# A list schedule that knows TensorE's tiling: each change of mode is charged, the mode at hand is preferred, and the order is drawn up anew

## The chip, the core and the metric

The kernel runs on one core of a Trainium2 chip. The metric is the device time of one launch in microseconds, 538.26 us in the median of three runs before the change. TensorE (PE in the profile, PEld its weight load), VectorE (DVE), ScalarE (ACT), GpSimd (POOL) and SyncE (SP, which issues the transfers) run side by side, each through its own list of instructions in the order in which the program gives them, and wait for one another by semaphores.

## What is computed

Shapes are 4 batches, 8 heads, 768 tokens, head size 48; the model width is 384 and the hidden width 1536. Cut to what matters, the reference is

```python
f = 1.0 / (1.0 + np.exp(-f_logit))
for t in range(S):                                   # attention with a gated state of 48x48
    state = f[:, :, t, :, None] * state + np.einsum('bhd,bhe->bhde', k[:, :, t], v[:, :, t])
    y[:, :, t] = np.einsum('bhd,bhde->bhe', q[:, :, t], state)
x = y.transpose(0, 2, 1, 3).reshape(B, S, H * D)
gate = sigmoid(sum(conv_w[k] * xp[:, k:k + S, :] for k in range(5)))   # causal, 5 taps
x = (gate * (x @ w_val)) @ w_out
xn = (x - mean) / sqrt(var + 1e-6) * g_ln
out = x + relu(xn @ w_ch1) @ w_ch2
```

The weights come in as 64-bit floats and are turned into pairs of 32-bit parts on the chip.

## The kernel before

The work is cut into 24 tiles of 128 tokens for the attention and 12 groups of 256 tokens for the dense layers. Every dense product is split into a high and a low part and made of three matmuls (`mm3`), in the form F32R: val (`ps<-xh,wv`), x1 (`ps<-wo,gh`), c1 (`ps<-nh,w`, 128x256) and c2 (`ps<-w,hidden`, 128x384). Of a tile of the attention TensorE does four things, each one block of instructions that the planner moves as a whole:

- T: transposes against an identity, `ps<-ident,kt` (and, ahead of the dense layer, `ps<-ident,xn`), 128 rows by 128 columns;
- a: `ps<-mv,kt`, scores of a chunk of 64 tokens, 48 rows by 64 columns of the array;
- d: `ps<-st,kn`, what a chunk adds to the state, 64 rows by 48 columns;
- y: `ps<-mv,st`, the output, 112 or 128 rows by 48 columns.

a, d and y use a part of the array only, and set TensorE to another tiling than T and the dense matmuls do. By the planner's classes a and d are one mode (at most 64 rows), y is a second, everything else is mode 0. Around these blocks DVE makes gates and running products (`gs`, `ft`, `kt`, `mv`, in `prep`), ACT copies the transposed keys (`kn`) and the scores, POOL masks the scores (`mv<-mv`). After d the state goes on through DVE (`sn<-sd,ps`), POOL (`sd<-sn,fc`) and a copy (`st<-sd`), and y of the same tile needs that copy.

Nothing of the order is written out by hand. `Kernel.record` records some 2,900 units (a block each) twice, and `Plan.schedule` sets the order: `forward` is a list scheduler which at each step takes the unit that can start first, and among equals the one of lowest rank. Ranks come from a backward pass, and the table `MOVED` then shifts the ranks of runs of units: (first unit, how many, by how much). Costs come from `price`, `transfer` and `wait`. In the old model every block on TensorE that isn't F32R pays `SWITCH` (0.12) once, whatever ran before it, and the transposes pay it too. The same order of one list then holds for all engines, the transfers on SP among them; places in PSUM (8 banks) are handed out as the order goes.

A word on stages: up to its first c1 matmul TensorE does seven tiles of the attention and one group of val and x1 besides transposes (128 rows of its list); from there the list mixes c1 and c2 of a group with the attention, val and x1 of later groups. Up to tile 7 (`TURNED`) q, k and f are transposed on TensorE (`ps<-ident,raw_f` and so on), later on DVE.

Of the kernel before, what the change touches and what calls it, by code (L numbers as in the profile page):

```python
# [49 lines left out]
FRONT = (-5, -4, -4, -2, -2, -1)  # L50
BIAS = 0.3
COLD = 1.25
WARM = 1.03
SWITCH = 0.12
TURNED = 8
REBIAS = 2.0**-112
TINY = 2.0**-60
# [5 lines left out]
FLIGHT = 8  # L63

MOVED = (
# [8 lines left out]
)  # L74


# [31 lines left out]
class Unit:  # L108


    def __init__(self, engine):
        self.costs = dict.fromkeys(engine.split("|"), 0.0)
        self.engine = next(iter(self.costs))
        self.calls = []
        self.delay = self.margin = 0.0
        self.deps = set()
        self.opens = None
        self.uses = set()
        self.port = False

# [12 lines left out]
class Plan:  # L133
# [43 lines left out]
    def record(self, engine, method, args, kw):  # L177
# [25 lines left out]
        for x, writes in [(x, False) for x in ins] + ([(out, True)] if on_chip(out) else []):  # L203
            r = self.region(x)
            if isinstance(r.name, int) and r.name not in u.uses:
                if not self.users[r.name]:
                    u.opens = r.name
                else:
                    u.deps.add(self.users[r.name][0])
                u.uses.add(r.name)  # L210
                self.users[r.name].append(me)
            ws, rs = self.access.setdefault(r.name, ([], []))
            for at, box in ws + (rs if writes else []):
                if at != me and (r.meets(box) or self.collide(r, at, u)):
                    first.deps.add(at)
            if writes:
                ws[:] = [(a, b) for a, b in ws if not r.covers(b)]
                rs[:] = [(a, b) for a, b in rs if not r.covers(b)]
                ws.append((me, r.box))
            elif (me, r.box) not in rs[-4:]:  # L220
                rs.append((me, r.box))
        if engine == "sync":
            return
        n = 1
        for _, k in out.ap[1:]:
            n *= k
        if engine == "tensor" and not u.costs["tensor"] and ins[0].dtype != F32R:
            u.costs["tensor"] = SWITCH
        wide = [x for x in ins if x.space != PSUM and x.ap[-1][1] > 1]
        single = method in ("tensor_scalar", "tensor_copy", "copy", "shifted") and out.space != PSUM  # L230
        u.port = method != "memset" and (len(wide) > 1 or (bool(wide) and (single or "gpsimd" in u.costs)))
# [13 lines left out]
    def price(self, engine, method, out, ins, n, args, kw):  # L245
        if engine == "tensor":
            if method == "transpose":
                return 0.105 * self.slow
            if ins[0].dtype == F32R:
                return (0.436e-3 * n + 0.006) * self.slow  # L250
            return (0.056 if n > D else 0.043) * self.slow
# [35 lines left out]
    def transfer(self, issued, u, out, in_):  # L287

        n = size = mybir.dt.size(out.dtype)
        for _, k in out.ap:  # L290
            n *= k
        run = size * min(out.ap[-1][1], in_.ap[-1][1])
        local = out.space == in_.space
        issued.costs = {"sync": 0.63 if out.ap[0][1] == 64 or local else 0.47}
        issued.delay = 0.5
        issued.margin = 0.0 if local else MARGIN
        u.costs = {"wire": n / run * (11.0 + (0.0595 if run < 1024 else 0.053 if run < 2048 else 0.0705) * run) / 16e3}
        u.delay = 1.2
        u.deps.add(len(self.units) - 1)

# [37 lines left out]
    def forward(self, deps, users, rank):  # L338
# [11 lines left out]
        homes = {}  # L350
        held = [len(x) for x in self.users]
        ends = [0.0] * len(held)

        def start(i, e):
            u = units[i]
            t = max(free[e], ready[i])
            if u.port and e in port:
                t = max(t, port[other[e]])
            if u.opens is not None:
                first = sorted(banks.values())  # L360
                spare = 1 if e == "vector" else 0
                t = max(t, first[spare]) if len(first) > spare else NEVER
            if e == "sync":
                t = max(t, free["wire"] - BACKLOG)
# [17 lines left out]
        while len(order) < len(units):  # L382
            best = None
            for e in ENGINES:
                for i in waiting[e]:
                    t = (start(i, e), ready[i] if e == "wire" else rank[i])
                    if (best is None or t < best[0]) and fits(i, e):
                        best = (t, i, e)
            (t, _), i, e = best
# [4 lines left out]
                waiting[x].remove(i)  # L394
            u.engine = e
            order.append(i)
            end[i] = free[e] = t + u.costs[e]
            if e == "sync":
                sent.append(i + 1)
            if u.port and e in port:  # L400
                port[e] = end[i] + 0.05
            if u.opens is not None:
                homes[u.opens] = min(banks, key=banks.get)
                del banks[homes[u.opens]]
            for r in u.uses:
                held[r] -= 1
                ends[r] = max(ends[r], end[i] + 0.17)
# [823 lines left out]
```

## Time and profile before

| | |
|---|---|
| median of three runs | 538.26 us (537.22 to 538.60) |
| the profiled execution | 538.87 us, of which its instructions span 537.2 us |
| mean granted TensorE clock | 0.99 |
| busy share of the span | PE 93%, PEld 89%, DVE 69%, ACT 50%, POOL 32% |
| costliest group | c1 `ps<-nh,w_hi`, 432 matmuls, 123.5 us busy |

Read a matmul's cost from the distance between two starts, not from its own duration: matmuls overlap in the array, a c1 matmul is shown with 0.28 us and the next one starts 0.11 us later. A timeline row `x32` stands for 32 instructions in a row of one kind; for a, d and y they are the 16 products of a block, each of which runs as two instructions on the chip.

### The profile page before, as it was taken

What the parts mean: (1) busy time and instruction counts of PE and PEld (TensorE: products, weight loads), DVE (VectorE), ACT (ScalarE), POOL (GpSimd) and SP (SyncE); (2) the same over time, 40 slices, a digit from 0 to 9 for tenths busy, and PEclk for the clock granted to TensorE, in tenths of its full rate; (3) what the DMA queues carried; (4) which work ended last, traced back from release to release, by engine and by line L of the source; (5) the groups of instructions that cost most, each with busy time, mean ns of one, the idle gap of its engine ahead of it and who ended that gap; (6) DMA issues with size and microseconds to landing.
All of it is one profiled execution on the core that took longest, in us unless ns stands there. A gap on an engine that the chain in (4) does not pass through costs nothing.

```text
span 537.2 us, 13413 instructions
## 1 busy us (share of the span) xinstructions
PE 501.3 (93%) x5272; PEld 477.9 (89%) x5272; DVE 369.1 (69%) x737; ACT 270.6 (50%) x591; POOL 169.5 (32%) x312
## 2 busy tenths in 40 slices
PE   2987689999999999999999999999999999999994
PEld 1776579999999999999989999999989999999993
DVE  5898989999884975874889733985793542543411
ACT  2598879995472453453486222543552542512210
POOL 3365676245340422230277001231421431300000
PEclk9998989999999999999999999999999999999998
DMA  6985786973454234133143610162110100000001
GB/s 137 177 172 106 190 214 173 234 227 83 103 145 94 51 85 92 39 100 70 38 114 73 149 47 1 31 156 60 24 39 9 23 31 2 9 31 1 29 1 35
DMA packets 94560, 45.60 MB, mean 85 GB/s; under 512 B 56341, under 2 KB 94485, under 8 KB 94490
## 3 DMA queue, kind: packets, MB, share of 16 engines
q1 hardware_dynamic: 94490, 44.67, 34.8%
q8 instruction: 43, 0.70, 0.6%
q14 instruction: 27, 0.22, 0.2%
HBM read 38.75 MB, written 4.72 MB: 81 GB/s over the span
## 4 chain that ended last, share of the span: by engine, by line
PE 71%; DVE 12%; DMA 4%; POOL 4%; ACT 3%; issue 2%; SPq 2%; DVEq 0%; POOLq 0%; ACTq 0%
PE ps L466 71%; DVE ps L466 4%; SPq L466 2%; POOL rs L466 2%; DVE mv L466 2%; DMA raw_q<-in_q 1%; DVE wt L466 1%; DMA xt<-x 1%; DMA stage<-in_moe_w_ch 1%; DVE gs L466 1%; ACT xn L466 1%; DVE bns L466 1%; DMA raw_f<-in_f_logit 1%; DMA out_x<-x 1%; DVE nl L466 1%
## 5 line engine op out<-in xcount | busy, mean ns | idle before, releaser
L466 PE MATMUL ps<-nh,w_hi 128*128 128x256 f32 x432 | 123.5, 286 | 0.4 <-DVE nl L466 0.3
L466 PE MATMUL ps<-nl,w_hi 128*128 128x256 f32 x432 | 121.1, 280 | 0.4 <-DVE nl L466 0.3
L466 PE MATMUL ps<-nh,w_lo 128*128 128x256 f32 x432 | 120.9, 280 | 0.0
L466 PE MATMUL ps<-w_hi,hidden_hi 128*128 128x384 f32 x288 | 99.3, 345 | 0.0
L466 DVE SCALAR_TENSOR_TENSOR hidden_lo<-ps,hidden_hi 128x512 fp32r<-128x512 f32 x72 | 49.2, 684 | 70.3 <-ACT hidden_hi L466 70.2
L466 PE MATMUL ps<-w_hi,hidden_lo 128*128 128x384 f32 x288 | 96.9, 337 | 0.0
L466 PE MATMUL ps<-w_lo,hidden_hi 128*128 128x384 f32 x288 | 96.8, 336 | 0.0
L466 ACT ACTIVATE hidden_hi<-ps 128x512 fp32r<-128x512 f32 x72 | 42.9, 595 | 85.7 <-PE ps L466 84.4
L466 PEld LDWEIGHTS ps<-nh,w_hi 128*128 128x128 f32 x432 | 81.3, 188 | 1.8 <-DVE nl L466 0.5
L466 PEld LDWEIGHTS ps<-nh,w_lo 128*128 128x128 f32 x432 | 82.1, 190 | 0.0
L466 PEld LDWEIGHTS ps<-nl,w_hi 128*128 128x128 f32 x432 | 81.2, 188 | 0.9 <-DVE nl L466 0.9
L466 DVE SCALAR_TENSOR_TENSOR ps<-xt,convw,ps 128x256 f32<-128x256 f32 x144 | 65.7, 483 | 3.5 <-ACT ps L466 1.8
L466 POOL TENSOR_SCALAR_AFFINE_SELECT mv<-mv 64x512 f32<-64x512 f32 x48 | 32.2, 671 | 86.6 <-ACT mv L466 84.9
L466 PEld LDWEIGHTS ps<-w_hi,hidden_hi 128*128 128x128 f32 x288 | 54.1, 188 | 1.1
L466 PEld LDWEIGHTS ps<-w_lo,hidden_hi 128*128 128x128 f32 x288 | 54.2, 188 | 0.0
L466 PEld LDWEIGHTS ps<-w_hi,hidden_lo 128*128 128x128 f32 x288 | 54.1, 188 | 0.0
L466 POOL TENSOR_TENSOR sd<-sn,fc 112x192 f32<-112x192 f32 x43 | 22.7, 529 | 69.8 <-DVE sn L466 54.9
L466 ACT COPY kn<-ps 64x192 f32<-64x192 f32 x96 | 30.1, 313 | 14.1 <-PE ps L466 12.9
L466 DVE TENSOR_TENSOR_SCAN gs<-ps,ends 128x511 f32<-128x511 f32 x24 | 29.1, 1214 | 9.3 <-ACT ps L466 8.9
L466 DVE TENSOR_TENSOR mv<-ps,ft 64x512 f32<-64x512 f32 x48 | 33.0, 688 | 2.5 <-PE ps L466 1.0
L466 PE MATMUL ps<-xh,wv_hi 128*128 128x256 f32 x108 | 32.7, 302 | 0.9 <-DVE gt L466 0.9
L466 PE MATMUL ps<-xl,wv_hi 128*128 128x256 f32 x108 | 31.4, 291 | 0.0
(102 smaller groups left out, 993.8 us busy)
## 6 DMA issues: line engine op xcount, KB each, us to landing
stage<-in_moe_w_ch SPq DMA_DIRECT2D x24, 384.0 KB, 4.5
st<-in_v SPq DMA_DIRECT2D x96, 48.0 KB, 2.5
out_x<-x SPq DMA_DIRECT2D x24, 192.0 KB, 1.9
raw_f<-in_f_logit SPq DMA_DIRECT2D x32, 96.0 KB, 2.3
raw_k<-in_k SPq DMA_DIRECT2D x32, 96.0 KB, 2.3
raw_q<-in_q SPq DMA_DIRECT2D x32, 96.0 KB, 2.4
raw_f<-in_f_logit SPq DMA_DIRECT2D x32, 80.0 KB, 2.2
raw_k<-in_k SPq DMA_DIRECT2D x32, 80.0 KB, 2.4
```

The costliest lines, as they stand in the source:

```text
L466: getattr(getattr(self.nc, engine), method)(*args, **kw)
```

## The change

The planner now carries the mode at hand through the forward pass. A block of a or d has mode 1, of y mode 2, all else 0, and a block whose mode differs from that of the block before it on TensorE pays 0.117 (into mode 0) or 0.092. Besides, the rank by which TensorE's blocks are compared gets `STAY` (3.0) added where the block would change the mode. `WARM`, the factor on all TensorE prices after the prologue, goes from 1.03 to 1.01, a transpose from 0.105 to 0.102; a transfer's price is divided by 14.5e3 instead of 16e3, so each counts 10% longer. `opens` becomes a list of banks (no block here opens two). `MOVED` is another table (50 entries for 47). No instruction on TensorE is added or removed; what moves is the order on all engines and, where a unit may run on either of two engines, the engine.

```diff
-WARM = 1.03
-SWITCH = 0.12
+WARM = 1.01
+TILING = (0.117, 0.092, 0.092)
+STAY = 3.0
 MOVED = (
-    (416, 8, -12), (2566, 20, -8), (22, 6, 5), (1533, 20, -20), (1524, 40, 8), (1231, 3, 8),
...
+    (0, 6, 8), (19, 1, -20), (48, 12, 8), (84, 1, 3), (100, 4, 12), (131, 3, -8), (134, 1, -7),
...
-        if engine == "tensor" and not u.costs["tensor"] and ins[0].dtype != F32R:
-            u.costs["tensor"] = SWITCH
+        if engine == "tensor" and method == "matmul" and ins[0].dtype != F32R:
+            u.mode = 1 if ins[0].ap[0][1] <= 64 else 2
...
-                return 0.105 * self.slow
+                return 0.102 * self.slow
...
-        u.costs = {"wire": n / run * (11.0 + (0.0595 if run < 1024 else 0.053 if run < 2048 else 0.0705) * run) / 16e3}
+        u.costs = {"wire": n / run * (11.0 + (0.0595 if run < 1024 else 0.053 if run < 2048 else 0.0705) * run) / 14.5e3}
...
+        mode = 0
+
+        def cost(i, e):
+            u = units[i]
+            return u.costs[e] + (TILING[u.mode] if e == "tensor" and u.mode != mode else 0.0)
+
+        def urgency(i, e):
+            if e == "wire":
+                return ready[i]
+            return rank[i] + (STAY if e == "tensor" and units[i].mode != mode else 0.0)
...
-                    t = (start(i, e), ready[i] if e == "wire" else rank[i])
+                    t = (start(i, e), urgency(i, e))
...
-            end[i] = free[e] = t + u.costs[e]
+            end[i] = free[e] = t + cost(i, e)
+            if e == "tensor":
+                mode = u.mode
```

Counted over TensorE's list from the first c1 matmul to the end of the planned work (the 128 rows ahead of it hold the same blocks in both kernels), neighbouring blocks stand so:

| neighbours on TensorE | before | after |
|---|---|---|
| dense, then a, d or y | 39 | 17 |
| T, then a, d or y | 11 | 9 |
| a, d or y, then dense | 42 | 19 |
| a, d or y, then T | 8 | 7 |
| y next to a or d | 1 | 7 |
| a next to d (one mode) | 1 | 15 |

The first place is on TensorE around tile 19's a block (`ps<-mv_115,kt_117`), with val on one side and c2 on the other.

```order
L466 MATMUL ps_163<-xh,wv_hi 128x256
L466 MATMUL ps_163<-xl,wv_hi 128x256
L466 MATMUL ps_163<-xh,wv_lo 128x256
L466 MATMUL ps_162<-mv_115,kt_117 64x64 x16
L466 MATMUL ps_157<-w_2_hi,hidden_hi 128x384
L466 MATMUL ps_157<-w_2_lo,hidden_hi 128x384
L466 MATMUL ps_157<-w_2_hi,hidden_lo 128x384
```

There the block of tile 19 stands alone. In the changed kernel the same block stands behind the same val, with d of its tile and y of tile 18 on its two sides:

```order
L480 MATMUL ps_161<-xh,wv_hi 128x256
L480 MATMUL ps_161<-xl,wv_hi 128x256
L480 MATMUL ps_161<-xh,wv_lo 128x256
L480 MATMUL ps_162<-st_113,kn_122 48x48 x16
L480 MATMUL ps_159<-mv_115,kt_117 64x64 x16
L480 MATMUL ps_161<-mv_114,st_112 48x64 x16
L480 MATMUL ps_164<-nh_148,w_4_hi 128x256
L480 MATMUL ps_164<-nl_150,w_4_hi 128x256
L480 MATMUL ps_164<-nh_148,w_4_lo 128x256
```

Three stretches of tiled work, each with dense work before and behind it, have become one.

The second place is on TensorE at tile 17: its d block is `ps<-st_113,kn_122`, its y block `ps<-mv_115,st_113`. Before, d stands behind y of tile 16, and 18 c1 matmuls and 6 c2 matmuls follow before y of tile 17:

```order
L466 MATMUL ps_162<-mv_114,st_112 48x64 x16
L466 MATMUL ps_157<-st_113,kn_122 48x48 x16
L466 MATMUL ps_161<-nh_147,w_4_hi 128x256
L466 MATMUL ps_161<-nl_149,w_4_hi 128x256
L466 MATMUL ps_161<-nh_147,w_4_lo 128x256
```

In the changed kernel 6 c2 matmuls (the last three are shown) and two blocks of transposes stand between that d and y of tile 17, and d and a of tile 18 follow:

```order
L480 MATMUL ps_164<-w_5_hi,hidden_hi 128x384
L480 MATMUL ps_164<-w_5_lo,hidden_hi 128x384
L480 MATMUL ps_164<-w_5_hi,hidden_lo 128x384
L480 MATMUL ps_163<-ident,kt_117 128x112 x4
L480 MATMUL ps_158<-ident,xn_146 128x128 x3
L480 MATMUL ps_162<-mv_115,st_113 48x64 x16
L480 MATMUL ps_164<-st_112,kn_121 48x48 x16
L480 MATMUL ps_157<-mv_114,kt_116 64x64 x16
```

The distance from d to y of one tile has become shorter by 18 matmuls of c1, and three tiled blocks stand in a row.

The third place is the start of DVE's list: `gs`, `ft`, `kt` and `mv` are steps of `prep` for tiles 0 and 1, `wt` and `xn_146` belong to the convolution's weights. Before:

```order
L466 SCALAR_TENSOR_TENSOR gs<-ps_157,ends 128x511
L466 TENSOR_SCALAR lows<-gs 128x8
L466 TENSOR_TENSOR kt_116<-ps_158,gs 128x512
L466 RECIPROCAL starts<-lows 128x8
L466 TENSOR_TENSOR fc_119<-gs,ps_157 128x8
L466 SCALAR_TENSOR_TENSOR ft<-ps_157,starts 128x512
L466 SCALAR_TENSOR_TENSOR wt<-ps_159,wt 5x384
L466 TENSOR_TENSOR mv_114<-ps_161,ft 64x4x2x64 x2
```

In the changed kernel:

```order
L480 SCALAR_TENSOR_TENSOR wt<-ps_157,wt 5x384
L480 COPY xn_146<-wt 5x3x48
L480 COPY xn_146<-wt 5x3x16
L480 COPY xn_146<-wt 5x3x48
L480 COPY xn_146<-wt 5x3x16
L480 SCALAR_TENSOR_TENSOR gs<-ps_159,ends 128x511
L480 TENSOR_SCALAR lows<-gs 128x8
L480 TENSOR_TENSOR fc_119<-gs,ps_159 128x8
L480 RECIPROCAL starts<-lows 128x8
L480 SCALAR_TENSOR_TENSOR ft<-ps_159,starts 128x512
L480 TENSOR_TENSOR kt_116<-ps_160,gs 128x512
```

The convolution's weights stand first, and `kt` of tile 0 stands behind `ft`. On SP the first load of k moves from the 8th transfer to the 12th, the first load of f stays the 7th, f for tile 2 moves from the 19th to the 21st, and q for tile 1 moves forward from the 22nd to the 15th.

## Rows read from the trace of the kernel before

**Rows 1.** The page's line of busy time, share of the span and instructions.

```profile
PE 501.3 (93%) x5272; PEld 477.9 (89%) x5272; DVE 369.1 (69%) x737; ACT 270.6 (50%) x591; POOL 169.5 (32%) x312
```

**Rows 2.** Busy time by stretch: length, engines' busy us (count), PEclk, DMA share, GB/s.

```profile
20.00:30.00 10.00, 8.41 (x167) 7.07 (x168) 8.03 (x17) 6.50 (x18) 5.06 (x11) 1.00 0.85 166
...
10.00:81.00 71.00, 55.32 (x844) 47.47 (x842) 63.94 (x131) 55.64 (x131) 39.75 (x63) 0.95 0.79 171
81.00:529.00 448.00, 443.88 (x4428) 428.98 (x4422) 299.28 (x593) 213.18 (x461) 125.67 (x224) 1.00 0.28 71
```

**Rows 3.** Timeline of PE at the first c1 matmul: start us, duration us, instruction.

```profile
81.05 0.38 PE L466 MATMUL ps<-nh,w_hi 128*128 128x256 f32 x1
```

**Rows 4.** Timeline of PE around a d block between c1 matmuls.

```profile
253.33 0.28 PE L466 MATMUL ps<-nl,w_hi 128*128 128x256 f32 x1
253.44 0.28 PE L466 MATMUL ps<-nh,w_lo 128*128 128x256 f32 x1
253.65 0.92 PE L466 MATMUL ps<-st,kn 64*48 64x48 f32 x32
254.50 0.38 PE L466 MATMUL ps<-nh,w_hi 128*128 128x256 f32 x1
254.72 0.29 PE L466 MATMUL ps<-nl,w_hi 128*128 128x256 f32 x1
```

**Rows 5.** Timeline of PE where an a block follows a d block.

```profile
394.02 0.92 PE L466 MATMUL ps<-st,kn 64*48 64x48 f32 x32
394.77 1.11 PE L466 MATMUL ps<-mv,kt 48*64 48x64 f32 x32
395.82 0.38 PE L466 MATMUL ps<-nh,w_hi 128*128 128x256 f32 x1
```

**Rows 6.** Timeline of PE where transposes stand between tiled blocks.

```profile
281.88 0.55 PE L466 MATMUL ps<-ident,xn 128*128 128x128 f32 x3
282.35 1.10 PE L466 MATMUL ps<-mv,st 112*48 112x64 f32 x32
283.39 0.60 PE L466 MATMUL ps<-ident,kt 112*128 112x112 f32 x4
283.92 0.92 PE L466 MATMUL ps<-st,kn 64*48 64x48 f32 x32
```

**Rows 7.** Timeline of PE where transposes stand between c2 matmuls.

```profile
251.08 0.55 PE L466 MATMUL ps<-ident,kt 112*128 112x112 f32 x4
251.40 0.42 PE L466 MATMUL ps<-w_hi,hidden_hi 128*128 128x384 f32 x1
251.66 0.33 PE L466 MATMUL ps<-w_lo,hidden_hi 128*128 128x384 f32 x1
251.83 0.33 PE L466 MATMUL ps<-w_hi,hidden_lo 128*128 128x384 f32 x1
```

**Rows 8.** Groups by line and form: count, busy us, mean ns, idle before them.

```profile
L466 POOL TENSOR_TENSOR sd<-sn,fc 112x192 f32<-112x192 f32 x43 | 22.7, 529 | 69.8 <-DVE sn L466 54.9 <-DVE lows L466 11.2 <-DVE fc L466 1.7
L466 DVE TENSOR_TENSOR sn<-sd,ps 112x192 f32<-112x192 f32 x44 | 15.2, 345 | 15.0 <-POOL sd L466 7.3 <-PE ps L466 6.4 <-ACT gh L466 1.1
L466 ACT COPY st<-sd 48x192 f32<-48x192 f32 x38 | 13.3, 351 | 24.0 <-POOL sd L466 23.7
```

**Rows 9.** PE's waits, whole span: for what, us in total, times, longest us.

```profile
PE ps L466 <- POOL mv L466: 0.9, 2, 0.4
```

**Rows 10.** Timeline of DVE near the start; in brackets idle time before and releaser.

```profile
13.48 0.52 DVE L466 SCALAR_TENSOR_TENSOR wt<-ps,wt 5x384 int32<-5x384 int32 x1
...
15.49 0.24 DVE L466 COPY xn<-wt 5x144 f32<-5x144 f32 x1
...
21.64 1.22 DVE L466 TENSOR_TENSOR_SCAN gs<-ps,ends 128x511 f32<-128x511 f32 x1 [1.83 <-ACT ps L466]
```

**Rows 11.** Timeline of SP's issues: two loads of k.

```profile
5.37 0.58 SPq L466 DMA_DIRECT2D raw_k<-in_k  x1
...
9.22 0.55 SPq L466 DMA_DIRECT2D raw_k<-in_k  x1
```

More of the change, by code (lines that the diff above doesn't have):

```diff
@@ L116, in __init__ @@
         self.deps = set()
-        self.opens = None
+        self.opens = []
+        self.mode = 0
         self.uses = set()
@@ L206, in record @@
                 if not self.users[r.name]:
-                    u.opens = r.name
+                    u.opens.append(r.name)
                 else:
@@ L358, in start @@
                 t = max(t, port[other[e]])
-            if u.opens is not None:
+            if u.opens:
                 first = sorted(banks.values())
-                spare = 1 if e == "vector" else 0
+                spare = len(u.opens) - (0 if e == "vector" else 1)
                 t = max(t, first[spare]) if len(first) > spare else NEVER
@@ L401, in forward @@
                 port[e] = end[i] + 0.05
-            if u.opens is not None:
-                homes[u.opens] = min(banks, key=banks.get)
-                del banks[homes[u.opens]]
+            for r in u.opens:
+                homes[r] = min(banks, key=banks.get)
+                del banks[homes[r]]
             for r in u.uses:
```

14 rows, old and new, of the table MOVED are left out of this document.

## The prediction

> **What bounds the kernel now.** I read the share of busy time first, then the busy time by stretch, then timelines of TensorE at the places where blocks of different kinds meet, then the waits. The reader is to see that TensorE has 93% of the span and nobody else over 69% [rows 1], and that this isn't spread evenly: from 81 to 529 us it is idle for 448.00 - 443.88 = 4.1 us, while from 10 to 81 us it is idle for 15.7 us and DVE is the fullest engine, with 63.94 of 71 us [rows 2]. The border is the first c1 matmul, at 81.05 us [rows 3]. So the kernel is two problems: a start of 81 us in which transfers and DVE set the pace, and 448 us in which the end moves only with TensorE's own work and with waits put into it. The change takes no matmul away, so what it can give in the long stretch is the time between blocks.
>
> **What a change of tiling costs.** Starts of c1 matmuls are 0.11 to 0.12 us apart; I take 0.115. In front of a d block the distance is 0.21 (253.44 to 253.65), so going in costs 0.095 [rows 4]. The d block takes 0.85 until the first matmul behind it (253.65 to 254.50) where c1 follows, and 0.75 (394.02 to 394.77) where an a block follows [rows 4, 5]: going out costs 0.10 at the border. Then the first matmul behind it holds up the second: 0.22 instead of 0.115 (254.50 to 254.72), 0.105 more [rows 4]. Out to dense work is 0.205 in all, and a round trip 0.30 us. Staying within a mode costs nothing that the d block followed by a shows.
>
> Transposes are in the dense mode but pay in another way. Four of them take 0.32 and the c2 matmul behind them 0.26 instead of 0.17, 0.41 together [rows 7]. Between y and d four of them take 0.53 (283.39 to 283.92) [rows 6], so the two sides cost 0.12 more than between dense matmuls; I put 0.05 on the way out and 0.07 on the way in. A y block takes 1.04 until the transposes behind it [rows 6]; nothing in the rows has a y block followed by its own mode, so I take the 0.10 of d at that border too. Out to transposes is then 0.15, in from transposes 0.07. A border between y and a or d I price at the same 0.10.
>
> **The sum for the long stretch.** The counts are those of the table with the change. Before: 39 x 0.095 + 11 x 0.07 + 42 x 0.205 + 8 x 0.15 + 1 x 0.10 = 3.7 + 0.8 + 8.6 + 1.2 + 0.1 = 14.4 us. After: 17 x 0.095 + 9 x 0.07 + 19 x 0.205 + 7 x 0.15 + 7 x 0.10 = 1.6 + 0.6 + 3.9 + 1.1 + 0.7 = 7.9 us. That is 6.5 us less, nearly all on the path, since only 4.1 us of this stretch are idle and so could hide it.
>
> Ten of the 15 new joints within a mode are a followed by d, the other way round from what rows 5 show. From below each costs 0 as there, from above the 0.10 of leaving the mode, so the saving lies between 5.5 and 6.5. I take 6.5, since the same two blocks meet in the row. The Trainium skill, "TensorEngine Tiling (Array Packing)", section Tiling Modes, says that a change of mode drains the engine while a change of tile does not, and lists 64x64 as one mode. By that rule a and d share it in either order and the sum stays 6.5; without it, it would be 5.5.
>
> **What the joined blocks cost in waits.** Blocks that stand together have less dense work between a step and the step that needs it. The tightest place that I find in the order is tile 17. Between its d and its y stand 6 c2 matmuls at 0.17 (251.66 to 251.83), four transposes (0.32) and three (0.47 between other modes, less here): 1.0 + 0.32 + at most 0.47 = 1.8 us [rows 6, 7]. Over the same time the state goes through sn (0.345), sd on POOL (0.529) and a copy (0.351), 1.2 us, or 1.6 if the two copies of a chunk run one behind the other [rows 8], plus four hand-overs between engines that these rows don't price. So y waits there for 0 to 0.5 us; I take 0.3. Everything on TensorE's list queues behind that y: d and a of tile 18, then c1. Elsewhere three blocks or 2 us and more lie between a step and its user, about what the kernel before lives on with its 4.1 us idle, so I leave those 4.1 us as they are. Both ways the size is open: the 4.1 could lose 1 us, or gain 2.
>
> **The start.** The 128 rows of TensorE ahead of the first c1 are the same blocks, so only idle time can change, and DVE's list decides most of it. Four terms. (1) The convolution's weights now stand in front of the first gs, where DVE otherwise waits for the first load of f: wt 0.52 and four copies of at most 0.24 [rows 10] leave the full part, 0.5 to 1.5 us, I take 1.3 less. (2) The first load of k is the 12th transfer and not the 8th. Before, the 8th was issued at 5.37 and the 13th at 9.22 [rows 11], so it comes up to 3.85 us later; DVE has ft (a scan of some 1.2 us, as gs [rows 10]) put in front of kt meanwhile. It then idles for 0 to 2.6 us, I take 1.3 more. (3) The wait of 1.83 us ahead of gs for tile 2 [rows 10] gets cover, since q for tile 1 is issued seven places earlier and so both mv of tile 1 can run there; but f for tile 2 is issued two places later. 0 to 1.8 less, I take 1.2. (4) Ahead of the second nl, which the first c1 needs, DVE has 142 instructions and not 139; by the mean of 63.94 / 131 = 0.49 us [rows 2] that is 0 to 1.5 more, I take 1.5, since DVE is the bound. Together -1.3 + 1.3 - 1.2 + 1.5 = 0.3, which four guesses can't tell from zero: I put the first c1 where it is, 0 us, with -3.3 and +3.6 as ends (the best and the worst of all four). The 10% on transfers and WARM change no duration on the chip, only the order that I have counted.
>
> **The result.** 538.87 - 6.5 + 0.3 + 0 = 532.7 us for the profiled execution. That one is 0.6 above the median of the runs, so the median after should be 532.1 us.
>
> **Rivals.**
>
> *The start gets better too.* For it: DVE idles for 7.1 us between 10 and 81 us [rows 2], and the convolution is taken out of the full part. Against it: the later k. With 2 to 3.3 us less the time is 529 to 530; with an idle microsecond less in the long stretch, 527.8.
>
> *The gain is eaten in part.* The later k and DVE's additional work come in full (+3.6), or the waits grow by 2 us and a with d costs 0.10 at each joint (+1.0). Then 535 to 536.5 us; with both together 539.
>
> *Slower: the joined blocks wait for their chains.* TensorE now goes into tiled work 26 times and not 50, and y in such a group needs POOL's masking of a and the state's chain. Where y waited for the mask before, the longest wait was 0.4 us [rows 9]. If each of the 26 groups waits that long, that is 10.4 us for a saving of 6.5, and the time is 542.2. The gain is gone from 0.25 us a group, and the kernel is slower by more than 0.3% from 0.31. Against it: blocks of several tiles are joined, so the y in a group is mostly not fed by the a and d next to it, and 4.1 us in 448 is little to begin with.
>
> *Slower: the clock falls in the joined stretches.* From 20 to 30 us TensorE ran little but transposes and tiled blocks, with 1.6 us idle, and had the upper level of its clock (2.4 GHz, granted 1.00) throughout [rows 2]. If the lower level (1.2 GHz) came instead for the 52 tiled blocks of the long stretch, each of some 0.85 us would take up to twice that, 44 us in all: 576. The Trainium skill, "TensorE: Matmul & The Clock Gate", section Part 1: The HAM clock gate, says that half rate is the default and activity releases it, which would speak against long stretches of small matmuls; by that rule the saving turns into a loss, by the row the clock stays up.
>
> **How the numbers follow.** A measurement of this kernel can tell about 0.3%, 1.6 us, from no change. The forecast, 530 to 535, gets 0.65; the better start, below 530, 0.17; the gain eaten in part, 535 to 536.6, 0.06, and up to no difference, 536.6 to 539.9, 0.07; waits that cost more than they save 0.03; the clock 0.02. So faster 0.88, same 0.07, slower 0.05. The range reaches down to a start and waits at nearly their best ends (538.3 - 6.5 - 3.3 - 1.0 = 527.5) and up to where waits and joints take 4 to 5 us: 527.5 to 537.0.
>
> **What would show it.** Right: the first c1 matmul within 3 us of 81; from there to the last c2 the time falls by 5 to 7 us while TensorE's idle time stays near 4 us; an a block behind a d block, and d behind a, follow 0.75 to 0.95 us after the one before started, without a hold-up behind them; distances at the remaining borders as in rows 4 to 7. Wrong: idle time before y for POOL's mv or for st that adds up to several us; the first c1 later than 84.6; a lower granted clock after 81 us; or a d behind a that costs as much as a c1 behind a, in which case tiling isn't what the border costs.

## The result, and the profile after

The changed kernel takes 531.96 us in the median of four runs (531.19 to 532.53), against 537.74 for the kernel before on the same chip: a ratio of 0.9891, interval 0.9869 to 0.9913. The forecast was 532.1, so the size came out too; but that it came out so closely is luck, for it is a sum of two errors. The long stretch gave 9.0 us where 6.5 were forecast, and the start took 1.75 us more where 0 was forecast. Both are read from one profiled execution of each kernel. They come to 7.25 us, as those two executions do (538.87 to 531.72), while the medians differ by 5.8; some 1.4 us of the sum is thus scatter between executions, which the traces can't place.

The windows of after, in the columns of [rows 2] (stretch, length, busy time of PE, PEld, DVE, ACT and POOL, clock, DMA share, GB/s):

```profile
10.00:81.00 71.00, 57.66 (x809) 51.22 (x810) 61.72 (x124) 52.34 (x119) 35.73 (x61) 0.88 0.70 150
82.80:522.80 440.00, 436.35 (x4426) 426.36 (x4422) 308.42 (x609) 215.20 (x464) 113.76 (x212) 1.00 0.30 75
```

The same stretch of the kernel before, from its first c1 matmul to its last c2:

```profile
81.00:530.00 449.00, 444.02 (x4428) 428.98 (x4422) 300.10 (x595) 213.18 (x461) 125.67 (x224) 1.00 0.28 71
```

TensorE does the same 4,426 to 4,428 instructions in 440.0 us and not 449.0. Its busy time falls by 7.7 us and its idle time by 1.3 (4.98 to 3.65). The clock is 1.00 in both. Ahead of 81 us the changed kernel looks worse: DVE is idle for 9.3 us of 71 and not 7.1, and the mean clock is 0.88, not 0.95.

The timeline of PE at the first c1 matmul, which answers to [rows 3]; in brackets idle time before and its releaser:

```profile
82.80 0.38 PE L480 MATMUL ps<-nh,w_hi 128*128 128x256 f32 x1
83.57 0.39 PE L480 MATMUL ps<-nl,w_hi 128*128 128x256 f32 x1 [0.38 <-DVE nl L480]
```

The first place of the change, tile 19's a block with d and y around it, on PE's timeline:

```profile
364.43 0.28 PE L480 MATMUL ps<-xh,wv_lo 128*128 128x256 f32 x1
364.64 0.92 PE L480 MATMUL ps<-st,kn 64*48 64x48 f32 x32
365.41 1.15 PE L480 MATMUL ps<-mv,kt 48*64 48x64 f32 x32
366.71 1.10 PE L480 MATMUL ps<-mv,st 112*48 112x64 f32 x32 [0.15 <-DVE gt L480]
367.74 0.39 PE L480 MATMUL ps<-nh,w_hi 128*128 128x256 f32 x1
367.96 0.28 PE L480 MATMUL ps<-nl,w_hi 128*128 128x256 f32 x1
```

From the last dense start to d it is 0.21 instead of 0.12, as in [rows 4], d is followed by a after 0.77 (0.75 in [rows 5]), and the second matmul behind the group is held up once (0.22) for three blocks.

The joint that the prediction had left open, an a block with d behind it, occurs ten times; at one of them PE's timeline has:

```profile
302.01 1.15 PE L480 MATMUL ps<-mv,kt 48*64 48x64 f32 x32
303.00 0.89 PE L480 MATMUL ps<-st,kn 64*48 64x48 f32 x32
303.81 0.44 PE L480 MATMUL ps<-w_hi,hidden_hi 128*128 128x384 f32 x1
```

The d block starts 0.98 us after the a block. In front of dense work an a block takes 1.04 to 1.05 although it stands behind a d there (348.77 to 349.81 below, and [rows 5]). And this d block takes 0.81 until the dense matmul, where one behind dense work takes 0.85 [rows 4].

The second place, tile 17 from its d to its y, and what follows:

```profile
344.17 0.92 PE L480 MATMUL ps<-st,kn 64*48 64x48 f32 x32
...
346.18 0.55 PE L480 MATMUL ps<-ident,kt 112*128 112x112 f32 x4
346.56 0.49 PE L480 MATMUL ps<-ident,xn 128*128 128x128 f32 x3
346.98 1.10 PE L480 MATMUL ps<-mv,st 112*48 112x64 f32 x32
348.01 0.92 PE L480 MATMUL ps<-st,kn 64*48 64x48 f32 x32
348.77 1.11 PE L480 MATMUL ps<-mv,kt 48*64 48x64 f32 x32
349.81 0.38 PE L480 MATMUL ps<-nh,w_hi 128*128 128x256 f32 x1
```

No bracket stands in front of y at 346.98: the chain through sn, sd and st, with durations close to those of [rows 8], fits under the 2.8 us between d and y.

### The profile page after: what moved, and what is told of

It reads as the page before. It is cut to its first block, busy times and chain, and to the rows that moved or that the text cites. A ratio compares the mean times of both kernels' runs of the same rounds, so it can differ in the third digit from the quotient of the medians.

```text
span 530.0 us, 13426 instructions
## 1 busy us (share of the span) xinstructions
PE 496.4 (94%) x5272; PEld 479.5 (90%) x5272; DVE 378.2 (71%) x751; ACT 272.7 (51%) x590; POOL 154.9 (29%) x300
## 4 chain that ended last, share of the span: by engine, by line
PE 74%; DVE 12%; ACT 4%; DMA 4%; issue 2%; POOL 2%; SPq 1%; DVEq 0%; ACTq 0%; POOLq 0%
PE ps L480 74%; DVE ps L480 4%; DMA stage<-in_moe_w_ch 2%; DVE gs L480 1%; DVE wt L480 1%; DVE mv L480 1%; ACT ps L480 1%; SPq L480 1%; DMA raw_f<-in_f_logit 1%; DVE ps L1031 1%; ACT wt L480 1%; DMA st<-in_v 1%; POOL rs L480 1%; DVE kt L480 1%; POOL sd L480 0%
## 5 line engine op out<-in xcount | busy, mean ns | idle before, releaser
L480 POOL TENSOR_SCALAR rs<-bna 128x1 f32<-128x1 f32 x24 | 6.2, 258 | 102.4 <-DVE bna L480 102.1
L480 PE MATMUL ps<-mv,kt 48*64 48x64 f32 x768 | 30.8, 229 | 1.3 <-DVE mv L480 1.1
```

The costliest lines, as they stand in the source:

```text
L480: getattr(getattr(self.nc, engine), method)(*args, **kw)
```

## The experiments

Each kernel ran in three rounds beside the kernel before, whose medians were between 536.1 and 537.7 in the five sets of runs (the last kernel in five rounds); ratios are to it. "Entries" are places in the long stretch where TensorE goes from dense work or transposes into tiled work (50 before, 26 after).

**Pulling joined blocks apart.** The changed order, with the next dense block put between any two tiled blocks that stand together; the other engines' lists stay.

```diff
+            if kinds[seq[p]] == "tiled" and kinds[seq[p + 1]] == "tiled":
...
+                    if kinds[seq[q]] == "dense":
+                        new = seq[: p + 1] + [seq[q]] + seq[p + 1 : q] + seq[q + 1 :]
```

> The changed kernel, with the next dense block put between any two tiled blocks that stand together on TensorE from the first c1 on; the lists of all other engines and the start are those of the changed kernel. TensorE goes into tiled work 49 times again (50 before the change, 26 after it). Theory (the gain is the price of the changes of mode): by the borders measured in the changed kernel, in from dense 0.13 us (0.094 at the border, 0.036 inside the block), out to dense 0.205, between modes 0.136, the counts (22 more in from dense, 21 more out to dense, 7 fewer between modes, 3 more at transposes) give 6.6 us more: 538.6 us, and 446 to 447 us from the first c1 to the last c2 instead of 440, with the first c1 still at 83 us. Rival (the gain comes from the new order on the other engines and from fewer waits, not from the modes): 532, with at most 1 us more.

It took 559.46 us, 1.0418 (1.0392 to 1.0444), where 538.6 was expected. The long stretch is 26 us longer. Added up over the distances between starts on PE, the borders cost 6.4 us more, of the 6.6 expected; the rest is mostly waits of dense matmuls that now come earlier than their operands (15.1 us idle for 3.65). The stretch, and the first of PE's waits in it (for what, us, times, longest):

```profile
82.80:548.60 465.80, 450.71 (x4425) 430.33 (x4422) 306.98 (x607) 214.41 (x464) 114.26 (x212) 1.00 0.28 71
```

```profile
PE ps L555 <- DVE hidden_lo L555: 2.7, 6, 0.8
PE ps L555 <- ACT nh L555: 2.4, 3, 1.2
```

So this run shows the border price at the borders themselves, but also that a local move on one engine's list costs more than the borders. Whether that comes from the other engines' lists, which were made for another order, was tried next.

**The same list on TensorE, everything else planned anew around it.**

```diff
+                    if e == "tensor" and self.fixed and i != self.fixed[0]:
+                        continue
```

> As the run with the tiled blocks put apart: the same list on TensorE, with 49 goings into tiled work. But the planner then drew up the lists of all other engines anew for that list, where they had been left as they were. Theory: the price of the modes (6.6 us over the changed kernel by the counts) and far fewer waits than in that run: 539 to 545 us from waits of 4 to 10 us. Rival (the blocks' neighbours matter little and the waits of that run are inherent to the list): 552 to 560 us.

563.97 us, 1.0503 (1.0451 to 1.0554), above even the rival's 552 to 560. The long stretch:

```profile
83.20:552.90 469.70, 451.23 (x4428) 432.45 (x4422) 310.56 (x609) 217.83 (x468) 107.50 (x206) 0.99 0.27 70
```

The waits don't go away when the other engines follow: TensorE idles for 18.5 us and not 15.1. That points to the list, on which dense blocks are taken too early. It isn't shown, though, since the planner followed with a table of shifts that was searched for another list, and what such a table is worth on its own list comes out below as some 14 us.

**Joining blocks in the kernel before.** Its order, with a lone tiled block moved later, behind up to six blocks, to the next tiled one (36 entries for 50).

```diff
+            if kinds[seq[p]] == "tiled" and kinds[seq[p - 1]] != "tiled" and kinds[seq[p + 1]] != "tiled":
...
+                    new = seq[:p] + seq[p + 1 : q] + [seq[p]] + seq[q:]
```

> The kernel before, with nothing changed but that a tiled block which stands alone on TensorE is moved back behind up to 6 dense or transpose blocks to the next tiled block, where dependences allow it; other engines' lists and the model as before. TensorE goes into tiled work 36 times instead of 50, with 9 borders between modes instead of 1. Theory: 9 fewer in from dense at 0.13, 5 fewer in from transposes at 0.106, 9 fewer out to dense at 0.205, 5 fewer out to transposes at 0.15, 8 more between modes at 0.136 make 3.2 us less, 534.5 us, with the start as before (first c1 at 81 us), less what the moved blocks wait or make others wait (up to 1 us). Rival (order of the other engines): 537.7, no change, or slower by waits.

560.90 us, 1.0442 (1.0411 to 1.0473), where 534.5 was expected: the opposite sign. The borders did fall by about 3 us, but the long stretch has 23 us idle for 5. PE's longest waits in it are for xn and gt, which are computed from what the y blocks give; besides, the clock fell to the lower level three times (mean 0.99):

```profile
79.70:552.00 472.30, 448.88 (x4426) 432.90 (x4422) 299.66 (x595) 212.84 (x461) 126.26 (x224) 0.99 0.26 67
```

```profile
PE ps L549 <- POOL xn L549: 4.6, 3, 2.4
PE ps L549 <- ACT gt L549: 3.7, 2, 1.9
```

This is the rival in which the joined blocks wait, at full size. So joining isn't free. The changed kernel's whole schedule was drawn up with the joining in it, and of such waits it has 0.2 us after 83 us, for gt; no run tests by itself that this is the reason.

**A tiled product by itself, and a plain one.** In the changed kernel one product of 8 columns is put ahead of the first c1 step of each of 72 blocks, once with 48 rows by 64 columns of the array and once with all of it; its result is overwritten.

```diff
+                if u == 0 and isinstance(self.nc, Plan):
-                    self.nc.mark = (ph[0:64, 0, 0:8], self.ident[0:48, 0:64], self.ident[0:48, 0:8])
+                    self.nc.mark = (ph[0:128, 0, 0:8], self.ident[0:128, 0:128], self.ident[0:128, 0:8])
```

> The changed kernel with its order untouched, and one tiny product added ahead of every c1 step's first matmul (72 in all): 48 rows by 64 columns of the identity times 8 columns, plain 32-bit, into the place that c1 then overwrites. It sets TensorE to the tiling of a and d and back. Theory (a change of tiling is what the borders cost): 72 round trips at 0.094 in, 0.10 out, 0.107 for the second matmul, and some 0.06 for the product itself (two instructions) make 0.36 us each, 26 us in all: 558 us, few waits more. Rival (the borders cost because plain 32-bit work meets F32R work, whatever the tiling): the same as the kernel with the full-array product in its place.

> As the kernel with the tiny products, but each uses the whole array: 128 rows by 128 columns of the identity times 8 columns, the same 72 places, plain 32-bit too. Theory (tiling is what costs): only what a transpose costs beside dense work, 0.03 until the dense matmul, 0.088 for the second one and some 0.06 for itself, 0.12 to 0.18 us each, 9 to 13 us in all: 541 to 545 us, 13 to 17 us below the other. Rival (any plain 32-bit product costs the same): 556 to 560 us, no difference to the other.

553.90 us (1.0319, 1.0289 to 1.0349; 558 expected) and 543.66 us (1.0135, 1.0111 to 1.0159; within the 541 to 545 expected). PE's timeline at one of the 72 places, the tiled product first and then the plain one in the other kernel:

```profile
101.43 0.28 PE L485 MATMUL ps<-nh,w_lo 128*128 128x256 f32 x1
101.64 0.28 PE L468 MATMUL ps<-ident 48*64 48x8 f32 x2
101.84 0.39 PE L485 MATMUL ps<-nh,w_hi 128*128 128x256 f32 x1
102.07 0.29 PE L485 MATMUL ps<-nl,w_hi 128*128 128x256 f32 x1
```

```profile
100.95 0.28 PE L485 MATMUL ps<-nh,w_lo 128*128 128x256 f32 x1
101.07 0.28 PE L468 MATMUL ps<-ident 128*128 128x8 f32 x2
101.21 0.36 PE L485 MATMUL ps<-nh,w_hi 128*128 128x256 f32 x1
101.41 0.28 PE L485 MATMUL ps<-nl,w_hi 128*128 128x256 f32 x1
```

By the medians of such places a tiled product costs 0.40 us in all and a plain one 0.22; going in is 0.09 against nothing, but the held-up second matmul is 0.22 against 0.20, so it is there without any change of tiling. The tiling's own part is 0.18 us a round trip (0.14 by the two totals, 10.2 us over 72). The rest, the product's own time in it, is what a plain 32-bit product costs here between F32R matmuls. Over the changed kernel the two totals are only 0.30 and 0.16 us a place: 18 of the 72 products stand behind transposes or tiled blocks and not behind dense work, and the long stretch's idle time shrank.

**The planner's model without its table.** Both models with `MOVED = ()`.

```diff
-MOVED = (
...
+MOVED = ()
```

> The kernel before with an empty table MOVED: what the old model gives without its search, to be set beside the new model without its search (545.9 us, 40 goings into tiled work; here 52). Theory (the model joins blocks, the search does the rest): 9 fewer in from dense at 0.13, 12 fewer out at 0.205, 3 fewer in from transposes, 4 more between modes make the new model 3.4 us better, so 549 us here, if the starts and waits are alike. Rival (the new model gives nothing, all comes from the newly searched table): 546 or less.

> The changed kernel with an empty table MOVED: what the new model gives without the search. TensorE goes into tiled work 40 times from the first c1 on. Theory (most of the joining is the search's, the model alone joins little, and its start is not tuned): between the two kernels in the long stretch, about 3 us above the changed kernel by its changes of mode (14 more in, 14 more out, 3 fewer between modes: 18 x 0.13 + 18 x 0.205 less 9 saved elsewhere, 3 to 4 us), so 443 to 444 us from first c1 to last c2, and a start at 84 to 88 us: 535 to 541 us. Rival (the new prices alone carry the gain): 532 to 533.

Old model 551.93 us (1.0292, 1.0262 to 1.0322; 549 expected), new model 545.92 (1.0160, 1.0143 to 1.0177; slower than the 535 to 541 expected). So the model alone is worth 6.0 us (7 by the ratios), and in either model the search of the table 14 to 16 more. Entries: 52 and 40. By the counts only some 3.4 us of the 6.0 are borders: the old model's order also idles for 12.5 us in its long stretch where the new one's idles for 8.7, and its first c1 comes 3.3 us earlier. These are one order of each model.

**The parts of the new model, without the table.** First without the preference for the mode at hand, then with the old price of transfers.

```diff
-STAY = 3.0
+STAY = 0.0
```

```diff
-        u.costs = {"wire": n / run * (11.0 + (0.0595 if run < 1024 else 0.053 if run < 2048 else 0.0705) * run) / 14.5e3}
+        u.costs = {"wire": n / run * (11.0 + (0.0595 if run < 1024 else 0.053 if run < 2048 else 0.0705) * run) / 16e3}
```

> The new model without search and without its preference for the mode at hand (STAY 0 and not 3): the charge per change of mode stays. In the list TensorE goes into tiled work 52 times in the long stretch and not 40, as often as in the old model without search. If it is the preference that joins the blocks and the joined blocks that give the model its 6.0 us (545.9 against 551.9), this kernel stands near the old model: 12 entries more at 0.40 us a round trip, of which the 0.22 for plain 32-bit work is also paid by blocks that stand between transposes, so 3 to 5 us, and the time is 549 to 551. Rival: the model's gain comes from its other numbers (the transfers' price, WARM, the charge itself), then it stays at 545 to 547. Second rival: a joined order waits more, so that without joining the time falls below 545.

> The new model without search, with the old price of transfers (bytes divided by 16e3 and not 14.5e3); everything else as in the changed model. TensorE goes into tiled work 38 times in the long stretch (40 with the new price). If the price of transfers is worth nothing by itself the time is 544.5 to 547.5. Rival: the new price was there to keep transfers from being scheduled too early, and without it TensorE and VectorE wait for loads in the first 85 us: first c1 matmul 2 us later or more than the 84.4 us of the model alone, and a time of 548 to 551.

558.37 us (1.0395, 1.0378 to 1.0412) and 540.25 us (1.0045, 1.0031 to 1.0059). The long stretch of three kernels without a table: the new model, then without the preference, then with the old price of transfers; each from its first c1 matmul to its last c2:

```profile
84.40:537.30 452.90, 444.23 (x4464) 429.26 (x4463) 306.85 (x601) 221.94 (x477) 117.19 (x212) 1.00 0.28 72
```

```profile
84.00:548.50 464.50, 450.18 (x4424) 432.32 (x4422) 301.81 (x587) 217.57 (x472) 124.00 (x218) 0.99 0.27 69
```

```profile
78.10:531.00 452.90, 445.09 (x4518) 430.04 (x4518) 310.16 (x606) 220.70 (x476) 118.62 (x211) 1.00 0.28 72
```

The preference is worth 11.6 us of the long stretch, with the start as it is; by itself, the charge per change of mode leaves the 52 entries of the old model. Half of the 11.6 is busy time (6.0) and half idle (5.6), so the expectation of 549 to 551 was too small mainly by the idle half; some of the busy half is the clock, which fell to the lower level three times (mean 0.99). By the border prices measured above, the 12 entries more are some 2 to 3 us of the 11.6; seven waits of 1.0 to 2.1 us make up 10.7 us of this order's idle time. The price of transfers changes nothing in the long stretch and costs 6.3 us at the start (78.1 to 84.4). That is the reverse of the rival that I had set against it, and with 540.25 the time also lies below the 544.5 to 547.5 expected. These are single orders, though, and other orders of the same planner lie several us apart, so these differences are shown for these lists and not as a rule.

**The table with the old price of transfers.**

> The changed kernel with its own table of shifts, and only the price of transfers undone (bytes divided by 16e3). If a table is worth something only on the list on which it was searched, it is lost here: TensorE goes into tiled work 35 times in the long stretch (26 in the changed kernel), and the time is that of an order without a search, 540 us (as the new model with this price and no table) to 550. Rival: the table's 14 us and the better start of the old price add up, first c1 matmul near 78 and a time of 526 to 529.

544.47 us, 1.0121 (1.0099 to 1.0144), first c1 at 85.0 and 35 entries, within the 540 to 550 expected: 4 us worse than the same model with no table at all. With one number of the model changed, this table of shifts has lost its worth.

**An earlier start.** The changed order with conv_w, then f, k and q of tiles 0 and 1 ahead of v and w_val on SP, and the convolution's transpose behind the first f's.

```diff
+        front = [nth("conv_w", 0), nth("f_logit", 0), nth("in_k", 0), nth("f_logit", 1),
+                 nth("in_q", 0), nth("in_k", 1), nth("in_q", 1)]
+        got = self.settled(order, engines, homes, "sync", front + [i for i in seq if i not in front])
...
+        new = seq[1:2] + seq[:1] + seq[2:]
```

> The changed kernel with its start reordered: on SP the convolution's weights, then f, k, f, q, k, q of tiles 0 and 1 go ahead of v and w_val; on TensorE the convolution's transpose stands behind the first f, on ACT the copy of convw behind the second sigmoid. Everything later as in the changed kernel. Theory (the start of the changed kernel is 1.75 us longer because the first f lands 5.2 us after its issue, behind w_val and v, where it took 3.3 before, so that DVE's first gs starts at 11.66 and not at 10.17 us): the first gs starts at 9 to 9.5 us, the first c1 comes 1 to 2.3 us earlier, the time is 529.7 to 531 us. Rival (the start is set later, by w_val and by TensorE's lower clock level from 33 to 44 us): first c1 at 82.5 to 84 us, time 532 or slower.

530.23 us in the median of five runs (527.96 to 530.67), 0.9874 (0.9858 to 0.9891), 1.7 us below the changed kernel, with overlapping intervals. In the profiled run, the fastest of the five, the first c1 stands at 80.16 instead of 82.80. The expectation had misread a load: the first two loads of f in the changed kernel took 3.2 and 4.1 us, and 5.2 is the time from the issue of the first, tile 1's, to the landing of the second, tile 0's.

**Tile 0's f first.** In that kernel, as in the changed one, the first load of f is that of tile 1; here the two are exchanged, as they were before the change, and both transposes of tile 0 go ahead of the convolution's.

```diff
-        front = [nth("conv_w", 0), nth("f_logit", 0), nth("in_k", 0), nth("f_logit", 1),
+        front = [nth("conv_w", 0), nth("f_logit", 1), nth("in_k", 0), nth("f_logit", 0),
...
-        new = seq[1:2] + seq[:1] + seq[2:]
+        new = seq[1:3] + seq[:1] + seq[3:]
```

> The kernel with the early start, now with the load of f that tile 0 needs ahead of that of tile 1 (in the changed kernel tile 1's is issued first, in the kernel before tile 0's), and the transposes of tile 0's f and k ahead of the convolution's. If the exchange of these two loads is what holds up the start, the transposes of f begin at 5 to 5.5 instead of 7.45, the first gs comes when DVE has finished the convolution's weights, at 7.4 to 7.8 instead of 9.26, and since the start is DVE's the first c1 comes 1 to 1.9 us earlier, at 78.3 to 79.2: 528.3 to 529.3 us in the median, 0.982 to 0.986 of the kernel before. Rival: the next load binds instead (f or k of tile 1, q), so the wait only moves to a later gs or mv, the first c1 stays at 79.8 to 80.4 and the time at 530.

529.54 us (528.42 to 530.02), 0.9840 (0.9825 to 0.9855): the best of all, 2.4 us below the changed kernel, but not by the way expected. The first gs does come as DVE gets free, at 7.42 and not 9.26. Then the gs of tile 2 waits longer, on DVE's timeline in the kernel with the early start and in this one:

```profile
9.26 1.22 DVE L554 TENSOR_TENSOR_SCAN gs<-ps,ends 128x511 f32<-128x511 f32 x1 [1.87 <-ACT ps L554]
...
21.46 1.22 DVE L554 TENSOR_TENSOR_SCAN gs<-ps,ends 128x511 f32<-128x511 f32 x1 [1.28 <-ACT ps L554]
```

```profile
7.42 1.22 DVE L554 TENSOR_TENSOR_SCAN gs<-ps,ends 128x511 f32<-128x511 f32 x1
...
22.60 1.22 DVE L554 TENSOR_TENSOR_SCAN gs<-ps,ends 128x511 f32<-128x511 f32 x1 [3.04 <-ACT ps L554]
```

What it waits for is on PE's timeline of this kernel, the load of tile 2's f:

```profile
21.30 0.66 PE L554 MATMUL ps<-ident,raw_f 128*128 128x128 f32 x4 [2.31 <-DMA raw_f<-in_f_logit]
```

So the rival's mechanism holds: one load brought forward makes a later one late, and in the profiled run (530.02, the slowest of the five) the first c1 stands at 81.8, later than either side had it. The median doesn't decide: 0.9840 is inside the theory's 0.982 to 0.986, and 529.54 lies between its 529.3 and the rival's 530.

## Why the prediction was right, and where its terms were off

The mechanism was right; that the median met the forecast so closely was luck, since the long stretch gave 2.5 us more than forecast and the start took 1.75 back. The sign that the long stretch falls by 5 to 7 us was missed with 9.0.

**The price of a change of tiling** was the right mechanism. Over the distances between starts on PE, the 22 dense-to-tiled borders that went away gave 2.03 us (forecast 22 x 0.095 = 2.1), the held-up second matmuls 2.49 (forecast 23 x 0.105 = 2.4), and ways out to dense work less the new joints 1.7 (forecast 2.3 - 0.6). With transposes some 0.4 more: 6.6 in all, against 6.5. The table with the change leaves out four joints of two blocks of one kind in the changed kernel (y with y twice, a with a, d with d: 26 + 7 + 15 is 48 of 52 blocks); at 0.04 to 0.05 us each they make it 6.4. A further 0.6 was not in the sum: the first pair inside a block is 0.034 to 0.049 us shorter where the block before had the same mode (0.4 of it in d blocks). The open joint, a followed by d, measures 0.05 us and d followed by a 0.04, against 0.14 to 0.15 from either to dense work or to y, so the upper of the two sums held. The bounds of 0.75 to 0.95 us that the text gave from start to start were for a behind d; d behind a comes after 0.98 because an a block is itself longer. The Trainium skill, "TensorEngine Tiling (Array Packing)", section Tiling Modes, has a change of mode drain the engine and a change of tile not; that a and d, 48x64 and 64x48, meet at 0.04 to 0.05 us in both orders and y meets either at 0.14 to 0.15 agrees with it.

**Why that price exists** I had partly wrong. I put all 0.30 us of a round trip down to tiling; the pair of inserted products shows that the hold-up of the second matmul, 0.105 of it, is nearly the same for a plain 32-bit product. The sum didn't suffer, since a joined block saves both.

**Waits of joined blocks.** Forecast: 4.1 us idle stays, and tile 17 adds 0.3. Tile 17 added nothing, and idle time over the stretch fell by 1.3 us; with waits that the windows count as busy, since a shown matmul overlaps the next start, some 2 us by the distances. This is the larger part of the surplus. PE's longest waits after 83 us are for others' work of the dense layers, not for POOL's masks:

```profile
PE ps L480 <- DVE hidden_lo L480: 1.0, 1, 1.0
PE ps L480 <- DVE wt L480: 1.0, 1, 1.0
```

A wait for POOL's mv occurs once, 0.4 us, in the start; twice before [rows 9]. The search seems to have made them small: without a table the same model idles for 8.7 us of this stretch (452.90 - 444.23), and the kernels in which blocks were parted or joined by hand added 11 and 18 us.

**The start** was the weak step, as the text said: four guesses with 0 as their sum. Measured: +1.75, inside the ends of -3.3 and +3.6 and inside the 3 us. Of the terms that were forecast, the one for DVE's additional work came out and the three for its waits did not add up. The terms, on DVE's timeline, beside [rows 10]:

```profile
7.40 0.55 DVE L480 SCALAR_TENSOR_TENSOR wt<-ps,wt 5x384 int32<-5x384 int32 x1 [1.24 <-ACT wt L480]
7.98 0.62 DVE L480 COPY xn<-wt 5x144 f32<-5x144 f32 x4
11.66 1.22 DVE L480 TENSOR_TENSOR_SCAN gs<-ps,ends 128x511 f32<-128x511 f32 x1 [3.07 <-ACT ps L480]
...
14.57 0.67 DVE L480 TENSOR_TENSOR kt<-ps,gs 128x512 f32<-128x512 f32 x1
...
24.38 1.22 DVE L480 TENSOR_TENSOR_SCAN gs<-ps,ends 128x511 f32<-128x511 f32 x1 [0.59 <-ACT ps L480]
```

(1) The convolution's weights did go into DVE's gap, as forecast, but the waits there are 1.24 + 3.07 = 4.31 us and not 4.01 as before. (2) The later k costs nothing: `kt` of tile 0 at 14.57 has no wait in front, ft covers it; forecast +1.3. (3) The wait ahead of gs for tile 2 went from 1.83 to 0.59, 1.2 less as forecast. What I missed is f of tile 0. I wrote of "the first load of f" as one and the same transfer, the 7th in both kernels; but the buffers have numbers, and by these the first load of f is now tile 1's. Tile 0's is issued at 5.63 and not 4.90, and takes longer. From the view of transfers, KB and us from issue to landing, in the kernel before and after:

```profile
raw_f<-in_f_logit SPq DMA_DIRECT2D x1, 192.0 KB, 3.3
```

```profile
raw_f<-in_f_logit SPq DMA_DIRECT2D x1, 192.0 KB, 4.1
```

So its transposes, and the first gs behind them, came 1.5 us later than before:

```profile
8.36 1.09 PE L466 MATMUL ps<-ident,raw_f 128*128 128x128 f32 x4 [8.36 <-DMA raw_f<-in_f_logit]
```

```profile
9.86 1.09 PE L480 MATMUL ps<-ident,raw_f 128*128 128x128 f32 x4 [0.66 <-DMA raw_f<-in_f_logit]
```

(4) DVE's additional instructions cost what was forecast. DVE's busy time up to the end of the second nl, before and after (stretch, length, busy time of DVE, clock, DMA share, GB/s):

```profile
0.00:80.86 80.86, 68.43 (x141) 0.96 0.77 165
```

```profile
0.00:83.52 83.52, 70.05 (x143) 0.90 0.70 150
```

It is busy for 1.6 us more (forecast +1.5) and idle for 13.5 and not 12.4, 1.0 more, where the first three terms had 1.2 less. Beside the late f of tile 0, which took back what the first term was to give, there are waits further on that no term had, such as 1.73 us ahead of the gs at 30.38. Together this nl ends 2.7 us later, and the first c1 only 1.75, because, other than the text had it, it doesn't need this nl: it starts before, and the second c1 matmul waits for it (the bracket at 83.57).

With +1.5 for f in place of the +1.3 for k the four terms would have come to 0.5, still short. In the two kernels with an earlier start DVE is about as busy up to that nl as in the changed one (70.4 and 70.2 us) and idles for 10.5 and 12.4, so there too the first c1 moves with DVE's idle time, and that changed with the order of the loads. How much of the 1.0 in the changed kernel is f of tile 0 they don't show, since an earlier first gs was in part given back at the gs of tile 2. That share and that of the clock (below) stay open.

**The rival of the clock** didn't happen: 1.00 in the joined stretches. The row that spoke against it is weaker than the text had it, though: in the start of the changed kernel the same kinds of blocks ran at the lower level for 10.2 us (last section). The rival of the joined blocks that wait didn't happen either, but the kernel with blocks joined by hand is that case, so a chance of 0.03 was small for what the counts in the order alone could tell.

## What to carry to other kernels

Price a border between kinds of work from distances between starts in the trace, on both sides of it and at the second instruction behind it, and count borders in the new order: that gave 6.4 to 6.6 of the 9.0 us. In the one pair of orders tried, a planner that prefers the kind at hand did better than one that only charges for the change. Don't join or part blocks by hand in a finished list: that cost 23 to 32 us here, also where the other engines were planned anew around it. The searched shifts did not survive a change of one number in the model, so search again after one, and in a start that is bound by loads, follow each load by the tile that it is for.

## What the runs showed of the hardware

- About half of what looks like the price of tiling comes with a plain 32-bit product on the full array too: 0.22 of 0.40 us for a round trip from c1 and back with a product of 8 columns, its own time included. The hold-up of the second matmul is nearly all of that kind (0.20 and 0.22 us where 0.12 is usual).
- 48x64 and 64x48 blocks meet at 0.04 to 0.05 us a joint in either order, where 0.14 to 0.15 stands between either and y, and a block behind its own mode is another 0.034 to 0.049 us shorter inside.
- The clock after a gap: in the changed kernel TensorE waited 2.56 us for `kt` up to 32.54, and then ran at the lower level (1.2 GHz) for 10.2 us of full work on transposes and tiled blocks, an a block taking 2.25 us to the next start and not some 1.0. At two later places, behind waits too, the lower level lasted 3.4 us, mostly on F32R matmuls (one is shown). From 20 to 30 us of the kernel before, the same kinds of blocks kept the upper level [rows 2], so these rows don't tell what brought it back.

```profile
29.40:33.40 4.00, 1.44 (x14) 1.15 (x12) 2.86 (x4) 3.87 (x9) 1.31 (x1) 1.00 0.13 29
33.40:43.60 10.20, 10.15 (x150) 8.77 (x150) 9.82 (x22) 8.17 (x19) 5.86 (x10) 0.50 0.75 142
47.00:50.40 3.40, 3.35 (x16) 3.38 (x17) 2.99 (x6) 1.60 (x5) 1.05 (x3) 0.50 0.94 211
```
